# Weight frequencies of an FFT-style convolution prepared in five groups instead of six

## The chip, the cores and the metric

The kernel runs on one core of a Trainium2 chip. Its engines are TensorE (PE in the profile; PEld is its weight load), VectorE (DVE), ScalarE (ACT), GpSimd (POOL) and SyncE (SP, which issues most DMAs). The metric is the device time of one execution in microseconds (us). Before the change it is 263.42 us, the median of three runs from 263.04 to 263.55.

## The reference

A 7x7 convolution over a 224x224 image with 96 channels in and 96 out, written as a product of Fourier transforms. It wraps around at the edges.

```
Xf = rfft2(x, axes=(1, 2))                     # x: (1, 224, 224, 96) bf16
Wf = rfft2(pad(w, 224 x 224), axes=(0, 1))     # w: (7, 7, 96, 96) bf16
Yf = einsum('bhwi,hwio->bhwo', Xf, Wf)
y  = irfft2(Yf, s=(224, 224), axes=(1, 2)).astype(bf16)
```

## The kernel before

**What it computes.** Only the image's height is transformed. It is cut into 8 blocks of 28 rows, each with 6 rows of overlap, and a block's transform has 17 frequencies (`NS`). Frequencies 0 and 16 are real (`REAL`); each of the others has two parts and a third plane, their difference, for a complex product of three multiplications. Along the width the 7 taps are applied directly, two output columns at a time, in a form with ten tap planes (`NTAP`: seven taps and three sums). So the transformed weights WF have 2 + 3 x 16 = 50 slots of 10 planes of 96x96, and a product is a chain of matmuls of 96 columns, with data planes as the stationary operand and WF as the moving one.

**Tiles and rounds.** The width is cut into 7 tiles of 32 columns, t = 0 to 6. `b_round(t, s, mid, end, ...)` (L532) multiplies frequency s of tile t. It takes two banks of the eight in PSUM: b0 is filled by 19 matmuls, then the round's fillers (`mid()`) stand in TensorE's order, then b1 by 14 matmuls. ScalarE copies a part of b0 to `tt_`; VectorE makes u from b0 and `tt_`, later v from `tt_` and b1; GpSimd adds u and v into yf, which SP sends to DRAM. u, v and `tt_` have two buffers each (`tv`, L782). An inverse transform of each tile follows later (`c_jobs`) and reads yf back as `tt`.

**J planes.** VectorE makes the sums and differences of the data that the matmuls load, three frequencies at a time (`JGB`), some rounds ahead, in three operations (`jit`, L479). Operation 1 serves b1, operation 2 the first matmuls of b0, operation 3 the last ones of b0. In the rounds in which planes are made, GpSimd's sum waits until they are done.

**Tiles 0 and 1 together.** The first loop runs r = 0 to 20. Frequency r of tile 0 and frequency r - 4 of tile 1 (`LAG`) alternate, and the slots in which fillers are placed are numbered k = 2r + t from r = 4 on. `add(a, b, jobs)` registers jobs for the slots a to b - 1, and `pace` (L787) takes equally many from the list in each, rounded up. The fillers are the weight groups and the forward transforms (`f_jobs`, matmuls of `xn` with Fm, in parts of 8, 5 and 4 frequencies) of tiles 1 and 2.

**Weight preparation.** `PGRP` (L33) says which frequencies are prepared together. `prep_jobs(gi)` (L349) has two kinds of job:
- `mk_(ob)`: matmuls into one bank. The stationary operand is the raw weights `wq`, read with a step of 96 elements: 98 rows (49 taps, for output channels o and o + 48) and 128 columns, of which 96 are the input channels. The moving operand is a part of Em, the matrix of the transform: 2 x 20 columns for each frequency of the group. One matmul gives output channels o and o + 48; 48 matmuls make a group. One evacuation then writes the bank into WF as bf16, on VectorE or ScalarE, whichever `evac` (L119) counts as less loaded.
- `diff(s)`: the third plane of a frequency as a difference of the first two, one VectorE operation of 960 elements. A group's differences follow its last matmul job.

Group 0 (frequencies 0 and 1) is prepared at the start and has a form of its own, 128 columns and four matmuls to a bank. The other groups of before have 3 frequencies: 120 columns, four matmuls and 480 columns to a bank, 12 banks. Group gi is registered for the slots of the group ahead of it (L807): `add(2 * PGRP[gi - 1][0], 2 * PGRP[gi - 1][1] - 1, ...)`. That gives slots 0 to 2 (group 1), 4 to 8 (group 2), 10 to 14 (group 3), 16 to 20 (group 4) and 22 to 26 (group 5), three jobs to a slot in the last four. When r passes the second last group's end by one (L838), `wq`'s memory is given to the inverse transform's buffers, and GpSimd clears one of them, GX.

Banks, and the buffers of u, v and `tt_`, are handed out when the program is built; an instruction waits until the last user of its bank or buffer is done. Each engine works through its instructions in the program's order. All operations are recorded by one helper, so that the profile shows L88 for nearly all of them; they are told apart by tile names.

Of the kernel before, what the change touches and what calls it, by code (L numbers as in the profile page):

```python
# [27 lines left out]
NB = 8  # L28
# [1 line left out]
NTAP = 10  # L30
TAPS = ((7, 8, 9, 6), (0, 2, 4, 6), (1, 3, 5))
NSLOT = 2 + 3 * (NS - 1)
PGRP = ((0, 2), (2, 5), (5, 8), (8, 11), (11, 14), (14, 17))  # L33
YGRP = ((0, 3), (3, 6), (6, 9), (9, 12), (12, 15), (15, 17))
SA = 13
NB4 = 4
# [14 lines left out]
def slot(s, part):  # L51
    return part if s == 0 else 2 + 3 * (s - 1) + part
# [3 lines left out]
def kernel(  # L56
# [7 lines left out]
    _, H, W, C = x.shape  # L64
# [8 lines left out]
    C2 = C // 2  # L73
# [31 lines left out]
    def bank():  # L105
        return pools["psb"].tile([128, 512], F32, name="pb")
# [5 lines left out]
    def apart(key, zone, r):  # L112
        for z, q in parts.setdefault(key, []):
            if z != zone and q.engine != r.ins.engine:
                tc.declare_no_dep(r.ins, q, reason="disjoint parts of one tile")
        parts[key].append((zone, r.ins))
        return r

    def evac(out_ap, in_ap, n):  # L119
        if tail[0]:  # L120
            return tail_evac(out_ap, in_ap, n)
        cv, ca = 180 + 1.0 * n, 160 + 0.85 * n
        if load["v"] + cv <= load["a"] + ca:
            load["v"] += cv
            return VE.tensor_copy(out=out_ap, in_=in_ap)
        load["a"] += ca
        return SE.copy(out=out_ap, in_=in_ap)

    def tail_evac(out_ap, in_ap, n):
        tail[0] += 1  # L130
        return VE.tensor_copy(out=out_ap, in_=in_ap) if tail[0] % 2 else SE.copy(out=out_ap, in_=in_ap)
# [29 lines left out]
    xh_bufs = [late[:, 2 * (XW + 32) + i * XHW:2 * (XW + 32) + (i + 1) * XHW] for i in range(2)]  # L161
    assert 2 * (XW + 32 + XHW) <= 8 * NTAP * C and NSLOT - 8 > slot(PGRP[-1][0], 0)

# [185 lines left out]
    def prep_jobs(gi):  # L349
        s0, s1 = PGRP[gi]  # L350
        ns = s1 - s0
        full = gi == 0
        ncol = (NSLOT_OF(s0, s1) if full else 2 * ns) * NTAP
        nb = C // NB
        hb = NB // 2
        nr = 512 // NB if full else ncol
        assert ncol <= nr and NB * nr <= 512 and C2 % hb == 0

        def mk_(ob):
            def f():  # L360
                pw = bank()
                pv_ = pw[:, 0:NB * nr].rearrange("p (k h q) -> p k h q", h=2, q=nr)
                ev = Em[:, :, slot(s0, 0):slot(s1 - 1, 2) + 1, :]
                ev = Em.rearrange("p h a t -> p h (a t)")[:, :, 0:nr] if full else ev.rearrange("p h (s r) t -> p h s (r t)", r=3)[:, :, :, 0:2 * NTAP]
                for k in range(hb):
                    o = ob * hb + k
                    TE.matmul(pv_[:, k], lhsT=wqx[0:PW2, o:o + 127 * C + 1:C], rhs=ev, start=True, stop=True)
                pv_ = pv_[0:C]
                o0, o1 = ob * hb, (ob + 1) * hb
                wv = WF[0:C, slot(s0, 0):slot(s1 - 1, 2) + 1]  # L370
                if full:
                    wv = wv.rearrange("i a t (h o) -> i (a t) h o", h=2)
                    apart(("W", gi), ob, evac(wv[..., o0:o1], pv_[..., 0:ncol].rearrange("i k h q -> i q h k"), NB * ncol))
                    return
                wv = wv.rearrange("i (s r) t (h o) -> i s (r t) h o", r=3, h=2)
                apart(("W", gi), ob, evac(wv[:, :, 0:2 * NTAP, :, o0:o1],
                      pv_.rearrange("i k h (s q) -> i s q h k", s=ns), NB * ncol))
            return f

        def diff(s):  # L380
            def f():
                load["v"] += 60 + C * NTAP / 1.92
                w0, w1, w2 = (WF[0:C, slot(s, r)].rearrange("i t o -> i (t o)") for r in range(3))
                VE.tensor_tensor(out=w2, in0=w0, in1=w1, op=ALU.subtract)
            return f
        return [mk_(ob) for ob in range(nb)] + ([] if full else [diff(s) for s in range(s0, s1) if s not in REAL])

    def NSLOT_OF(s0, s1):
        return slot(s1 - 1, 2) + 1 - slot(s0, 0)
# [381 lines left out]
    for f in prep_jobs(0):  # L771
        f()
# [30 lines left out]
    def add(a, b, jobs):  # L803
        qs.append([a, b, jobs, len(jobs)])

    for gi in range(1, len(PGRP)):
        add(2 * PGRP[gi - 1][0], 2 * PGRP[gi - 1][1] - 1, prep_jobs(gi))  # L807
    for t in range(2):
# [10 lines left out]
    for r in range(NS + LAG):  # L819
# [10 lines left out]
        for p in range(3):  # L830
            if r == SH2[p + 1] + 1 - (p == 2):
# [5 lines left out]
                add(2 * r, 2 * r + (8, 7, 5)[p], fj[0] + fj[1])  # L837
        if r == PGRP[-2][1] + 1:  # L838
            assert not any(q[2] for q in qs[:len(PGRP) - 1])
            wtmp_cm.__exit__(None, None, None)  # L840
# [10 lines left out]
        for t in range(2):  # L851
            s = r - LAG * t
# [79 lines left out]
    for i, (j, h) in enumerate(order):  # L932
# [3 lines left out]
        k = i + 8 - LF  # L936
# [38 lines left out]
```

## Time and profile before

| | |
|---|---|
| median of three runs | 263.42 us |
| the profiled execution | 263.23 us |
| its span in the trace | 261.5 us |
| granted TensorE clock | 1.00 |
| TensorE's first to last weight-preparation matmul | 15.6 to 74.3 us |
| matmuls out of `wq` | 48 of 128 columns, 240 of 120 |
| evacuations 96x480 into WF | 51 on ScalarE (586 ns), 9 on VectorE (642 ns) |
| differences `WF<-WF` on VectorE | 14, 744 ns each |
| HBM traffic | 160 GB/s over the span |

Times are counted from the span's start. A group row gives busy time, mean length of one instruction, and the idle time ahead of them with what ended it. In a timeline a row is a run of like instructions of one engine: start, length, and in brackets the idle time ahead of it. Matmuls are pipelined and a row of them ends with the drain of the last one, so rows overlap; how long a matmul occupies TensorE is read from the start of one row to the start of the next.

### The profile page before, as it was taken

The page shows a single profiled execution, that of the slowest core. Times are in us where ns is not written, and L with a number is a line of the kernel's source. Part 1 is how long each engine was busy: PE and PEld are TensorE (multiplying, and loading weights), DVE is VectorE, ACT ScalarE, POOL GpSimd, SP SyncE. Part 2 cuts the span into 40 slices and gives each one's busy share as a digit, 9 for nine tenths or more (in the row PEclk, how much of TensorE's full clock was granted, in tenths as well). Part 3 has the DMA queues.
Part 4 walks back from the last instruction along what each step waited for, and adds up shares of the span by engine and source line. Part 5 has one row for each costly group of instructions (what it writes and reads, how often), then busy time and mean ns, then how long its engine had stood idle before and what let it go on. Part 6 is the DMA issues. An engine that isn't in the chain of part 4 may idle for free.

```text
span 261.5 us, 12201 instructions
## 1 busy us (share of the span) xinstructions
PE 251.8 (96%) x5156; PEld 233.9 (89%) x5156; DVE 213.9 (82%) x455; ACT 198.0 (76%) x499; POOL 106.7 (41%) x172
## 2 busy tenths in 40 slices
PE   8999998999999999999999999999999999999982
PEld 3679998999999999999999989998999999999861
DVE  5659999898878889877977797777978889889982
ACT  5548997678885667997988879988798886666662
POOL 7784223435546533432243313543143222555621
PEclk9999999999999999999999999999999999999999
DMA  6848010721112399997978469797969853495145
GB/s 171 238 136 205 23 49 3 231 89 50 46 52 88 99 274 144 271 275 200 300 207 238 127 184 262 204 241 181 288 215 207 221 174 133 132 174 169 53 115 177
DMA packets 41416, 43.44 MB, mean 166 GB/s; under 512 B 30836, under 2 KB 33104, under 8 KB 41362
## 3 DMA queue, kind: packets, MB, share of 16 engines
q1 hardware_dynamic: 41044, 41.98, 58.5%
q8 instruction: 40, 0.66, 1.2%
q0 software_dynamic: 192, 0.52, 0.7%
q10 hardware_dynamic: 126, 0.17, 0.2%
q14 instruction: 14, 0.11, 0.1%
HBM read 22.09 MB, written 19.66 MB: 160 GB/s over the span
## 4 chain that ended last, share of the span: by engine, by line
PE 84%; DVE 4%; issue 4%; ACT 3%; POOL 3%; POOLq 0%; DVEq 0%; ACTq 0%
PE pb L88 84%; POOL ct L88 2%; ACT WF L88 1%; DVE xf L88 1%; DVE J L88 1%; POOL yf L88 1%; ACT xf L88 1%; DVE wq L88 1%; DVE u L88 0%; DVE v L88 0%; DVE yf L88 0%; ACT tt L88 0%; ACT J L88 0%; ACT tt__5413 L88 0%; ACT tt__1159 L88 0%
## 5 line engine op out<-in xcount | busy, mean ns | idle before, releaser
L88 PE MATMUL pb<-WF,J 96*128 96x96 bf16 x2782 | 160.4, 206 | 0.1
L88 PEld LDWEIGHTS <-J 96*128 96x128 bf16 x2782 | 136.0, 98 | 8.2 <-DVE u L88 1.5
L88 POOL TENSOR_TENSOR yf<-v,u 128x384 bf16<-128x384 f32 x70 | 69.1, 1002 | 127.2 <-issue 69.1
L88 ACT CAST xf<-pb 96x408 bf16<-96x408 f32 (+2 forms) x147 | 68.8, 486 | 9.1 <-PE pb L88 7.3
L88 PE MATMUL pb<-WF,xf 96*128 96x96 bf16 x991 | 61.4, 206 | 0.8 <-ACT xf L88 0.5
L88 DVE TENSOR_TENSOR J<-xf 96x1824 bf16<-96x1824 bf16 (+1 forms) x82 | 56.9, 732 | 0.1
L88 PEld LDWEIGHTS <-xf 96*128 96x128 bf16 x991 | 48.8, 98 | 1.4 <-ACT xf L88 0.6
L88 PE MATMUL pb<-Fm,xn 118*128 118x136 bf16 (+3 forms) x640 | 45.5, 199 | 1.4 <-DVE u L88 0.8
L88 PEld LDWEIGHTS <-xn 118*128 118x128 bf16 x640 | 30.5, 97 | 1.8 <-issue 1.8
L88 PE MATMUL pb<-tt,Gm 102*84 102x384 bf16 (+1 forms) x132 | 32.1, 326 | 0.0
L88 ACT CAST WF<-pb 96x480 bf16<-96x480 f32 (+1 forms) x57 | 28.4, 576 | 4.6 <-PE pb L88 4.5
L88 ACT CAST yo<-pb 84x384 bf16<-84x384 f32 (+1 forms) x65 | 27.8, 483 | 2.9 <-PE pb L88 2.9
L88 ACT CAST J<-pb 84x384 bf16<-84x384 f32 (+1 forms) x65 | 28.0, 484 | 2.5 <-PE pb L88 2.5
L88 DVE TENSOR_TENSOR J<-J 96x912 bf16<-96x912 bf16 (+2 forms) x41 | 22.8, 555 | 0.0
L88 PE MATMUL pb<-wq 98*128 98x120 bf16 (+1 forms) x288 | 21.4, 226 | 0.1
L88 PEld LDWEIGHTS <-wq 98*128 98x128 bf16 x288 | 19.4, 148 | 0.6 <-issue 0.6
L88 POOL TENSOR_TENSOR xn<-v,u 128x384 bf16<-128x384 f32 x12 | 10.9, 924 | 9.4 <-DVE J L88 6.4
L88 DVE CAST WF<-pb 96x480 bf16<-96x480 f32 (+1 forms) x15 | 8.8, 613 | 4.2 <-PE pb L88 4.2
L88 PE MATMUL pb<-wu 128*128 128x512 bf16 x39 | 11.0, 444 | 1.1 <-DVE ct L88 1.1
L88 PEld LDWEIGHTS <-Gm 102*84 102x84 bf16 (+1 forms) x132 | 11.1, 117 | 0.8
L88 DVE TENSOR_TENSOR yf<-v,u 128x384 bf16<-128x384 f32 x20 | 11.2, 558 | 0.7
L88 ACT COPY xf<-xf 96x816 bf16<-96x816 bf16 (+3 forms) x18 | 10.3, 630 | 0.0
(406 smaller groups left out, 252.8 us busy)
## 6 DMA issues: line engine op xcount, KB each, us to landing
scr<-yf SPq DMA_DIRECT2D x30, 288.0 KB
xn<-in_x_dram SPq DMA_DIRECT2D x12, 672.0 KB
tt<-scr SPq DMA_DIRECT2D x24, 336.0 KB
out_dram<-yo SPq DMA_DIRECT2D x12, 252.0 KB
out_dram<-J SPq DMA_DIRECT2D x12, 252.0 KB
tt<-scr SPq DMA_DIRECT2D x6, 288.0 KB
WF<-in_x_dram SPq DMA_DIRECT2D x2, 672.0 KB
scr<-yf SPq DMA_DIRECT2D x6, 192.0 KB
```

Source lines behind the costliest of these rows:

```text
L88: r = fn(*a, **k)
```

## The change

`PGRP` has five groups instead of six: frequencies 8 to 11 and 12 to 16 take the place of three groups of 3. `prep_jobs` computes the number of matmuls to a bank from the moving columns: 3 of 160 columns (480 in the bank, 16 banks) for the group of 4, and 2 of 200 columns (400 in the bank, 24 banks) for the group of 5. Groups 0 to 2 come out as they were. By L807 the group of 4 falls into slots 10 to 14, with 16 matmul jobs and 4 differences, and the group of 5 into slots 16 to 22, with 24 matmul jobs and 4 differences, four jobs to a slot in both. `wq`'s memory is given away at r = 13 instead of 15.

```diff
-PGRP = ((0, 2), (2, 5), (5, 8), (8, 11), (11, 14), (14, 17))
+PGRP = ((0, 2), (2, 5), (5, 8), (8, 12), (12, 17))
...
-        nb = C // NB
-        hb = NB // 2
         nr = 512 // NB if full else ncol
-        assert ncol <= nr and NB * nr <= 512 and C2 % hb == 0
+        hb = 512 // (2 * nr)
+        nb = C2 // hb
+        assert ncol <= nr and C2 % hb == 0
...
-                pv_ = pw[:, 0:NB * nr].rearrange("p (k h q) -> p k h q", h=2, q=nr)
+                pv_ = pw[:, 0:2 * hb * nr].rearrange("p (k h q) -> p k h q", h=2, q=nr)
...
-                    apart(("W", gi), ob, evac(wv[..., o0:o1], pv_[..., 0:ncol].rearrange("i k h q -> i q h k"), NB * ncol))
+                    apart(("W", gi), ob, evac(wv[..., o0:o1], pv_[..., 0:ncol].rearrange("i k h q -> i q h k"), 2 * hb * ncol))
...
-                      pv_.rearrange("i k h (s q) -> i s q h k", s=ns), NB * ncol))
+                      pv_.rearrange("i k h (s q) -> i s q h k", s=ns), 2 * hb * ncol))
```

## The prediction

> **What bounds the kernel now.** I read the page's busy shares first, then the same shares by stage, then TensorE's timeline inside the stage that the change touches, then VectorE's timeline beside it.
>
> ```profile
> PE 251.8 (96%) x5156; PEld 233.9 (89%) x5156; DVE 213.9 (82%) x455; ACT 198.0 (76%) x499; POOL 106.7 (41%) x172
> ```
>
> ```profile
> 38.60:53.64 15.04, 14.28 (x345) 14.16 (x343) 13.29 (x26) 9.66 (x24) 4.98 (x5) 1.00 0.44 127
> 53.64:65.62 11.98, 11.88 (x267) 11.76 (x265) 10.62 (x22) 10.23 (x24) 5.93 (x6) 1.00 0.14 51
> 65.62:78.16 12.54, 12.50 (x283) 12.41 (x281) 10.34 (x21) 10.02 (x24) 5.91 (x6) 1.00 0.11 41
> ```
>
> TensorE (PE) sets the end: nearly full in every stage, clock 1.00, and after this stage (78 to 247 us) its timeline has hardly a gap. So what TensorE gains or loses before 78 us should come out at the end one for one. The second reading is the warning: VectorE (DVE) is 82 to 89% busy in these three stages. A busy share is no price, but a queue that full has little room for work that arrives in a lump.
>
> The stage in TensorE's timeline, then VectorE's:
>
> ```profile
> 67.23 0.93 PE L88 MATMUL pb<-WF,J 96*128 96x96 bf16 x18
> 68.00 0.50 PE L88 MATMUL pb<-WF,xf 96*128 96x96 bf16 x8
> 68.34 0.46 PE L88 MATMUL pb<-WF,J 96*128 96x96 bf16 x7
> 68.64 0.92 PE L88 MATMUL pb<-wq 98*128 98x120 bf16 x12
> 69.39 0.40 PE L88 MATMUL pb<-Fm,xn 118*128 118x64 bf16 x8
> 69.82 0.93 PE L88 MATMUL pb<-WF,J 96*128 96x96 bf16 x18
> ```
>
> ```profile
> 51.87 2.10 DVE L88 TENSOR_TENSOR WF<-WF 96x960 bf16<-96x960 bf16 x3
> 53.90 0.54 DVE L88 SCALAR_TENSOR_TENSOR v<-tt__1501,pb 128x384 f32<-128x384 f32 x1
> ```
> The columns are start, length, engine, operation, output<-input, shape, count. The first six rows are one round: 18 + 8 + 7 = 33 matmuls of 96 columns, the round's share of weight preparation (`wq`, three banks of four matmuls), then pieces of the next tile's transform (`xn`). A row's length holds the drain of its last matmul, so spacing is read from start to start. The last two show that three differences of weight planes (`WF<-WF`) hold VectorE for 2.03 us before it can empty round 14's second bank. I count rounds as the kernel counts slots: k = 2r + tile.
>
> **1. TensorE's work.** Spacings: 120 columns 0.75 us / 12 = 62.5 ns (68.64 to 69.39); 136 columns 60 ns (three from 99.39 to 99.57); 384 columns 165 ns (two from 105.31 to 105.64); 96 columns 42.6 ns (18 from 67.23 to 68.00). The line through 136 and 384 (0.423 ns a column) gives 120 columns 53.2 ns, so the weight matmuls are 9 ns above it. Group 0 tells why: 48 of 128 columns took 3.03 us (15.62 to 18.65), 63.1 ns, so 8 columns more cost 0.6 ns where the line asks for 3.4. The weight load sets the spacing; its group's mean is 148 ns against 98 ns for loads from J or xn. Once the matmul is longer than the load, it is the line that counts: 160 columns 70.2 ns, 200 columns 87.1 ns. Both shapes are absent from this trace, so these are estimates.
>
> Removed: 144 x 62.5 = 9.00 us (three groups of 48). Added: 48 x 70.2 + 48 x 87.1 = 3.37 + 4.18 = 7.55 us. Gain 1.45 us. Bounds: if the 9 ns excess stayed, 48 x (79.5 + 96.4) = 8.44 us, gain 0.56; if spacing stayed at 62.5 ns, gain 3.0. I take the line, since its two ends bracket both widths.
>
> The Trainium skill (TensorE: Matmul & The Clock Gate, "Weight-path perf modes — Fast Weight Load (FWL) and DoubleRow") speaks against any gain here: it has the fast load on for 128 weights not in fp32, with a column step up to 1,024 elements, and this load's step is 96. By it the old matmuls would already sit on the line (144 x 53.2 = 7.66 us) and the gain would be 0.1 us. The trace disagrees: 62.5 ns and 148 ns against 98.
>
> **2. Evacuations.** 36 of 480 elements become 16 of 480 and 24 of 400. On ScalarE (ACT) three of 480 take 1.47 us with 0.59 for one, so 0.445 us apart; two of 320 take 0.77 with 0.43 for one, 0.335 apart; 400 lies at 0.39 between. 36 x 0.445 = 16.0 becomes 16.5 us, and the built program puts 36 of the 40 on ScalarE. Their output now goes in runs of 3 and 2 elements instead of 4. No row here has such a run; in contiguous rows and runs of 4 the length follows the element count alone (84x384 contiguous 484 ns, 96x400 494, 96x408 500). I take no penalty; below nothing is excluded, since no run shorter than 4 can be an easier write; the upper end is in the rivals.
>
> **3. What moves.** Rounds 10 to 13 prepare 48 matmuls as before, but in four banks each instead of three. All of group 4 falls into rounds 16 to 21 (8 matmuls, four banks each), rounds 22 to 25 lose their 12 each. The differences come four at a time: in round 14 (three before) and in round 22 (before: three in round 20, two in round 26). The GpSimd (POOL) memset of GX moves from 15 to 13 in the frequency loop: 0.56 us on an engine that is 41% busy. SP's transfers keep their order. Until round 22 TensorE therefore carries more, 3.37 - 3.0 + 4.18 - 3.0 = +1.55 us; the 3.0 us back come after it.
>
> **4. New waits.** I followed banks and buffers through the built program's instruction order, with durations of before (u 0.27 us apart, v 0.46, a difference 0.68; the two first J operations 1.32, or 1.63 to 1.88 beside a POOL sum as at 55.09 and 40.65; the third 0.54). All of these are estimates.
> - Round 10: the fourth bank moves the round's second half onto the bank that VectorE's yf sum empties at 40.73 us; TensorE would be there at 40.5. +0.3.
> - Round 11: TensorE already waits 0.76 us for u (43.48). The bank in question is now asked for two banks earlier, but freed at the same time. +0.1.
> - Round 16: the second half's bank is emptied by round 14's v, which stands behind four differences. TensorE arrives at 54.9, v ends at about 55.7. +0.8. Queued behind that v are u, v, round 15's J planes and, through them, GpSimd's sums (they wait for planes).
> - Round 18: a u behind those planes; 0.4 in place of the 0.3 of before (58.67 to 58.94). +0.1, and 0.1 of small ones.
> - Rounds 22 to 27: the largest. J planes for round 27 are made in round 24. Before, the VectorE queue between round 21's planes and these held only u and v, and it idled:
>
> ```profile
> 71.99 0.36 DVE L88 SCALAR_TENSOR_TENSOR u<-pb,tt__2113 128x192 f32<-128x192 f32 x1 [0.51 <-ACT tt__2113 L88]
> 73.02 0.56 DVE L88 SCALAR_TENSOR_TENSOR v<-tt__2113,pb 128x384 f32<-128x384 f32 x1 [0.66 <-PE pb L88]
> 73.49 1.40 DVE L88 TENSOR_TENSOR J<-xf 96x1824 bf16<-96x1824 bf16 x2
> ```
>
> (The bracket is the idle time ahead of the row and its cause: 0.51 + 0.66 us, so the planes were not late.) Now it holds planes 1.9, u 0.3, four differences 2.7, v, u, v 1.2, a wait for GpSimd's sum to free u 0.3, u, v 0.7, the next planes' first two 1.4: 8.5 us, starting 0.7 us after TensorE's round 21 ends, so 9.2. TensorE, lightened of its `wq` matmuls, reaches round 27 after four rounds of 1.64 and one of 1.41: 8.0 us. It waits 1.2 us.
>
> Sum: -1.45 + 0.3 + 0.1 + 0.8 + 0.2 + 1.2 = +1.15; the 0.2 us wait at 69.82 (69.39 + 8 x 28.75 ns, the spacing from 67.00 to 67.23, = 69.62) falls away: **+0.95 us**. After round 27 VectorE has no differences left and TensorE has no slack to give the time back. The profiled execution took 263.23 us (span 261.5 and 1.7 around it), 0.19 below the median 263.42; so 264.2 for it and **264.4** for the median.
>
> **Rivals.**
> - *Faster: the waits are hidden.* If VectorE reached round 14's v and round 24's planes 1 us sooner, only part 1 stays: -1.45 + 0.2 of small waits, 262.2. It decides at round 27: the planes must be ready 8.0 us after round 21's end instead of 9.2. For it: TensorE is 96% busy and VectorE had 1.2 us idle there. Against: the differences are 2.7 us.
> - *Even.* Round 16's wait is halved, round 27's only 0.6 us: 263.4.
> - *Short writes cost.* Rounds 18 to 21 give ScalarE 0.31 (tt) + 4 x 0.39 + 0.47 (xf) = 2.34 us against TensorE's 33 x 42.6 ns + 8 x 87.1 ns + 0.23 = 2.33. With no slack, 0.1 us more per evacuation is 0.4 us a round, 1.6 us in all: 266.0.
> - *Spacing keeps its excess*, 0.56 instead of 1.45 gained: up to 265.3. The Trainium skill's rule (fast load on) would leave no work gained, 265.8; with the 62.5 ns against it I give that 0.02, inside this case.
> - *The change does nothing it says*: excluded; the built program has 240 weight loads from `wq` where there were 288, and 64 evacuations into WF outside group 0 where there were 60.
>
> **Chances.** Forecast (264.0 to 265.0) 0.42; short writes 0.10; spacing 0.10; even 0.14; faster 0.24. Within 0.2% means within 0.53 us, about what a measurement here can tell from no change: same 0.14, faster 0.24, slower 0.62. The range takes most of the faster case and the short writes: 262.1 to 266.2. The slower cases alone: 264.0 to 266.2.
>
> **What would show it.** Part 1: twelve `wq` matmuls of 160 columns 0.84 us, eight of 200 columns 0.70 us, start to start. Part 2: the 96x400 casts near 494 ns. Part 4: TensorE waits for VectorE at two places, some 0.8 us eight matmuls of 200 columns into the stage (for a v) and some 1.2 us six rounds after the last `wq` (for J). If neither is there, the forecast fails and the time is near 262.2.

## The result and the profile after

The changed kernel takes **269.99 us** (median of six executions, 268.60 to 272.06) against 263.26 us before (six, 262.75 to 263.55): a ratio of 1.0264, 95% interval 1.0233 to 1.0295. That is 6.7 us slower; forecast was 264.4, with 266.2 as the upper end. The profiled execution took 268.60 us (span 266.8), 5.37 more than that of before.

The busy shares of the page, then the shares by stage. The stage is cut where TensorE stands at the same work as in the three rows of before: the `xf` matmuls ahead of round 10's weight matmuls, those weight matmuls of round 16, the `xf` matmuls of round 22, those of round 28.

```profile
PE 252.9 (95%) x5108; PEld 233.7 (88%) x5108; DVE 215.1 (81%) x456; ACT 203.7 (76%) x502; POOL 107.0 (40%) x172
```

```profile
38.60:56.29 17.69, 15.67 (x346) 15.11 (x343) 14.08 (x27) 15.21 (x27) 4.96 (x5) 1.00 0.40 117
56.29:72.25 15.96, 14.62 (x268) 13.60 (x265) 11.55 (x25) 14.19 (x32) 6.93 (x7) 1.00 0.11 40
72.25:83.74 11.49, 9.73 (x235) 9.47 (x232) 10.70 (x20) 5.35 (x13) 3.95 (x5) 1.00 0.07 27
```

The columns are the stretch and its length, then busy time and count of TensorE, its weight loads, VectorE, ScalarE and GpSimd, then clock, DMA share and GB/s. On the page nothing seems to happen: TensorE 251.8 us before and 252.9 after, 96 and 95% of the span. By stage the loss is plain. The stretch up to round 16 has 346 matmuls where it had 345, but lasts 17.69 us instead of 15.04, and ScalarE's busy time there rises from 9.66 to 15.21 us while its count rises from 24 to 27. The second takes 15.96 us instead of 11.98, with 268 matmuls where it had 267 and ScalarE busy for 14.19 us instead of 10.23; the third, with its `wq` matmuls gone, comes 1.05 us shorter (11.49). The clock is 1.00 throughout.

TensorE's timeline of the changed kernel, all rows of the stage at which the view shows a wait (start, length, shape, count, idle time ahead and what ended it):

```profile
43.41 0.60 PE L88 MATMUL pb<-wq 98*128 98x160 bf16 x6 [0.57 <-ACT WF L88]
44.17 0.38 PE L88 MATMUL pb<-wq 98*128 98x160 bf16 x3 [0.15 <-ACT WF L88]
...
55.83 0.33 PE L88 MATMUL pb<-WF,xf 96*128 96x96 bf16 x4 [1.10 <-DVE WF L88]
...
57.99 0.93 PE L88 MATMUL pb<-WF,J 96*128 96x96 bf16 x18 [0.78 <-DVE v L88]
...
76.64 0.33 PE L88 MATMUL pb<-WF,xf 96*128 96x96 bf16 x4 [0.78 <-DVE WF L88]
...
82.12 0.34 PE L88 MATMUL pb<-WF,J 96*128 96x96 bf16 x4 [0.98 <-DVE J L88]
```

The two waits that were forecast are there, 0.78 us for a v at round 16 and 0.98 us for J planes at round 27. So are waits for casts and for differences, which were not. ScalarE's timeline shows why, first one row of before, then the changed kernel:

```profile
40.69 1.47 ACT L88 CAST WF<-pb 96x480 bf16<-96x480 f32 x3
```

```profile
40.69 3.43 ACT L88 CAST WF<-pb 96x480 bf16<-96x480 f32 x4
...
50.47 3.55 ACT L88 CAST WF<-pb 96x480 bf16<-96x480 f32 x4
53.74 0.70 ACT L88 CAST xf<-pb 96x512 bf16<-96x512 f32 x1
54.26 0.49 ACT L88 ACTIVATE tt__1509<-pb 128x288 f32<-128x288 f32 x1
...
58.36 2.11 ACT L88 CAST WF<-pb 96x400 bf16<-96x400 f32 x4
```

Before, three casts of 96x480 took 1.47 us. Here four take 3.43 and 3.55 us, where 4 x 0.445 + 0.14 = 1.92 would be in line. The four of 96x400 come every 0.49 us, with 0.39 to be expected from their element count. Behind the second four of 96x480 the `tt` of round 14 is late (54.26), and VectorE stands idle for 1.69 us until it comes, where it was 0.58 us before. VectorE's row of before, then of the changed kernel:

```profile
51.60 0.36 DVE L88 SCALAR_TENSOR_TENSOR u<-pb,tt__1501 128x192 f32<-128x192 f32 x1 [0.58 <-ACT tt__1501 L88]
```

```profile
54.85 0.36 DVE L88 SCALAR_TENSOR_TENSOR u<-pb,tt__1509 128x192 f32<-128x192 f32 x1 [1.69 <-ACT tt__1509 L88]
```

**The theory** after this reading (A): the casts now write runs of 3 and 2 bf16 elements, and such short runs are slow; the lateness runs from ScalarE through `tt` to u, the differences and v. Rivals: PSUM is read in another step and that is slow (C); or the four differences in a lump do all of it and the casts are late only behind them (B).

### The profile page after: what moved, and what is told of

It reads as the page before. It is cut to its first block, busy times and chain, and to the rows that moved or that the text cites. A ratio compares the mean times of both kernels' runs of the same rounds, so it can differ in the third digit from the quotient of the medians.

```text
span 266.8 us, 12109 instructions
## 1 busy us (share of the span) xinstructions
PE 252.9 (95%) x5108; PEld 233.7 (88%) x5108; DVE 215.1 (81%) x456; ACT 203.7 (76%) x502; POOL 107.0 (40%) x172
## 4 chain that ended last, share of the span: by engine, by line
PE 73%; DVE 7%; ACT 7%; issue 4%; DMA 4%; SPq 2%; POOL 1%; DVEq 0%; ACTq 0%
PE pb L88 73%; ACT WF L88 5%; DVE J L88 2%; DMA wq<-in_w_dram 2%; DVE WF L88 2%; SPq L88 2%; DMA wq<-wq 1%; DVE v L88 1%; ACT xf L88 1%; DVE xf L88 1%; POOL yf L88 1%; DVE u L88 0%; DVE yf L88 0%; ACT tt L88 0%; ACT tt__1159 L88 0%
## 5 line engine op out<-in xcount | busy, mean ns | idle before, releaser
L88 POOL TENSOR_TENSOR yf<-v,u 128x384 bf16<-128x384 f32 x70 | 69.8, 1010 | 131.9 <-issue 69.7
L88 ACT CAST xf<-pb 96x408 bf16<-96x408 f32 (+3 forms) x146 | 69.1, 492 | 8.7 <-PE pb L88 6.9
L88 ACT CAST WF<-pb 96x480 bf16<-96x480 f32 (+1 forms) x59 | 35.7, 748 | 4.7 <-PE pb L88 4.6
L88 PE MATMUL pb<-wq 98*128 98x120 bf16 (+3 forms) x240 | 21.0, 234 | 1.2 <-ACT WF L88 0.7
L88 PEld LDWEIGHTS <-wq 98*128 98x128 bf16 x240 | 18.3, 145 | 2.2 <-issue 2.1
L88 DVE CAST WF<-pb 96x480 bf16<-96x480 f32 (+1 forms) x17 | 10.9, 679 | 4.2 <-PE pb L88 4.1
(404 smaller groups left out, 252.9 us busy)
```

Source lines behind the costliest of these rows:

```text
L88: r = fn(*a, **k)
```

## The experiments

Profiled executions start their first preparing matmul at 15.6 to 18.0 us, as the first DMAs land, and that goes straight through to the end. So profiles are compared by a **stretch**: from the second block of preparing matmuls (the first 20 of 120 columns) to the start of the 25 `J` matmuls of round 27. Before it is 77.09 - 20.55 = 56.54 us. All versions beside each other (ratios with 95% intervals, each against the kernel before on the same chip):

| version | median us | ratio | stretch us |
|---|---|---|---|
| before | 263.26 | 1 | 56.54 |
| changed | 269.99 | 1.0264 [1.0233, 1.0295] | 62.12 |
| `contig` | 266.07 | 1.0121 [1.0079, 1.0163] | 58.01 |
| `changed_pairs` | 265.86 | 1.0118 [1.0071, 1.0166] | 58.03 |
| `runs2` | 267.27 | 1.0174 [1.0147, 1.0202] | 60.15 |
| `spread` | 269.54 | 1.0255 [1.0221, 1.0289] | 61.85 |
| `old_slots` | 269.74 | 1.0258 [1.0210, 1.0306] | 60.40 |
| `contig_old_slots` | 264.52 | 1.0057 [1.0037, 1.0076] | 56.37 |
| `pairs_old_slots` | 264.89 | 1.0068 [1.0044, 1.0092] | 56.43 |
| `pairs_early` | 266.11 | 1.0122 [1.0077, 1.0168] | 58.22 |
| `pairs_no_differences` | 262.99 | 0.9994 [0.9979, 1.0008] | 55.67 |
| `pairs_pool4` | 268.47 | 1.0211 [1.0188, 1.0234] | 60.37 |
| `pairs_pool2` | 268.51 | 1.0206 [1.0181, 1.0231] | 58.22 |
| `before_pairs` | 263.19 | 0.9993 [0.9970, 1.0017] | 56.59 |

In the three versions with `old_slots` in their names a wait of 1.19 us follows in round 28, after the stretch. `before_runs3` and `before_runs1` ran once each and stand in their own section. A stretch is one profiled execution; a median can differ from its profile by more than a microsecond, so that small differences are read from the stretches and not from the medians.

### The writes alone: `contig`

```diff
-                wv = wv.rearrange("i (s r) t (h o) -> i s (r t) h o", r=3, h=2)
-                apart(("W", gi), ob, evac(wv[:, :, 0:2 * NTAP, :, o0:o1],
+                if ns > 3:
+                    z = 2 * hb * 2 * NTAP
+                    wo = wv.rearrange("i (s r) t o -> i s (r t o)", r=3)[:, :, ob * z:(ob + 1) * z].rearrange("i s (q h k) -> i s q h k", h=2, k=hb)
...
+                apart(("W", gi), ob, evac(wo,
```

The groups of 4 and 5 are written as runs of 120 and 80 elements. The weights land at other places than the products expect, so this version does not compute the convolution; its work is the same.

> The changed kernel, but each bank of the groups of 4 and 5 is written into WF as runs of 120 or 80 neighbouring elements instead of 3 or 2: same reads from PSUM, same counts, same engines, same order (the weights land at permuted places, so the output is not the reference's). Theory A, short write runs slow ScalarE's evacuations: the casts of 480 fall from 0.81 to about 0.45 us start to start, those of 400 from 0.49 to about 0.40, and the time comes to the forecast made without a penalty, about 264.4 us (263.8 to 265.5). Theory C, the wider step between PSUM reads (640 and 800 bytes instead of 480) slows them: casts and time as in the changed kernel, 269 to 270. Theory B, only the placement of the differences and the denser rounds: 269 to 270 as well, with the same casts.

ScalarE's casts in `contig`:

```profile
41.00 1.92 ACT L88 CAST WF<-pb 96x480 bf16<-96x480 f32 x4
...
56.16 1.66 ACT L88 CAST WF<-pb 96x400 bf16<-96x400 f32 x4
```

Four casts take 1.92 us, the value in line with before, with the changed kernel's read of PSUM. C falls, and B as the only cause: the differences still come four at a time, yet the stretch shrinks by 4.1 us and the time by 3.9. The median, 266.07 us, still lies above the range that A had given (263.8 to 265.5), so short writes are not the whole of the loss. What TensorE still waits for in `contig`:

```profile
43.79 0.60 PE L88 MATMUL pb<-wq 98*128 98x160 bf16 x6 [0.68 <-DVE u L88]
...
55.79 0.93 PE L88 MATMUL pb<-WF,J 96*128 96x96 bf16 x18 [0.21 <-DVE v L88]
...
58.94 0.33 PE L88 MATMUL pb<-WF,J 96*128 96x96 bf16 x4 [0.25 <-DVE u L88]
...
72.85 0.33 PE L88 MATMUL pb<-WF,xf 96*128 96x96 bf16 x4 [0.54 <-DVE WF L88]
...
78.34 0.34 PE L88 MATMUL pb<-WF,J 96*128 96x96 bf16 x4 [0.99 <-DVE J L88]
```

### What a short run costs: `before_runs3`, `runs2`, `before_runs1`

`before_runs3` puts 3 matmuls into a bank in place of 4 in before's last three groups; `runs2` puts 2 instead of 3 into a bank in the changed kernel's group of 4; `before_runs1` lets before's last three groups write the two halves of the channels innermost, which makes every element a run of its own. The names behind # are added here.

```diff
-        hb = NB // 2
+        hb = 3 if gi > 2 else NB // 2                                   # before_runs3
...
-        hb = 512 // (2 * nr)
+        hb = 2 if ns == 4 else 512 // (2 * nr)                          # runs2
...
-                wv = wv.rearrange("i (s r) t (h o) -> i s (r t) h o", r=3, h=2)
+                wv = wv.rearrange("i (s r) t (h o) -> i s (r t) o h", r=3, h=2)   # before_runs1
```

> The kernel before with three instead of four matmuls to a bank in groups 3 to 5: 16 casts of 360 elements in runs of 3 for 12 of 480 in runs of 4, PSUM step 480 bytes as before. By the length of 320 (0.335) and 480 elements (0.445) a cast of 360 would come every 0.36 us. Theory A: it takes clearly more, 0.55 to 0.65 us, and the time rises by some us. Theory C: 0.36 us, time within 1 us of before.

> The changed kernel with two instead of three matmuls to a bank in the group of 4: 24 casts of 320 elements in runs of 2, all starting on a multiple of 4 bytes, for 16 of 480 in runs of 3, half of which start in the middle of such a word. If odd runs are what costs (A, by alignment): 0.40 us each, 9.6 us for 12.9, and 2 to 3 us less than the changed kernel: 266.5 to 268. If every run costs the same extra time whatever its length (A, by count: 160 runs in a cast in both): 0.335 + 0.36 = 0.70 us each, 16.7 us for 12.9, and slower than the changed kernel: 272 or more.

> Complete kernel: the kernel before, where in groups 3 to 5 (fill 10 on) the 36 evacuations of 480 elements write single elements, 48 elements apart, in place of runs of 4; the read of PSUM takes the same pairs of steps in the other order. A look at the cost of single elements. If the cost goes by writes that do not fill and start on 4 bytes (runs of 2: 1.21 ns an element; runs of 3, of which every other one is off the 4 bytes: 1.68): about 2.3 to 3 ns an element, a spacing of 1.1 to 1.5 us on ScalarE, and 275 to 290 us. If the cost goes by the number of runs alone at the 2.4 ns a run that runs of 2 show: 2.4 ns an element, 1.15 us, the same to a measurement; if by bytes alone: 0.45 us and 263 us. Runs of 3 at 1.68 above runs of 2 at 1.21 speak against cost by the number of runs alone.

ScalarE in `before_runs3`, in `runs2` and in `before_runs1`:

```profile
41.73 2.66 ACT L88 CAST WF<-pb 96x360 bf16<-96x360 f32 x4
```

```profile
40.93 2.53 ACT L88 CAST WF<-pb 96x320 bf16<-96x320 f32 x6
```

```profile
41.06 6.67 ACT L88 CAST WF<-pb 96x480 bf16<-96x480 f32 x3
```

The spacing on ScalarE, start to start and as a mean, is 0.60 us for 360 elements in runs of 3 and 0.80 for 480 in the changed kernel, 0.39 for 320 and 0.487 for 400 in runs of 2, some 2.1 for 480 single elements, 0.445 for 480 in runs of 4. For one element: 1.7 ns in runs of 3, 1.2 in runs of 2, some 4.4 alone, 0.93 in runs of 4. For one run: 5.0 ns for 3 elements, 2.4 for 2, 4.4 for 1 and 3.7 for 4. A run of 3 is dearer than a run of 2 and than a run of 4, so it is neither a price for each run nor one for each element.

The place of a run counts too. The last two groups of `before_runs3` are all on ScalarE, 16 casts each. In both, the casts of the channels from 6, 15, 30 and 39 come 0.69 to 0.76 us ahead of the next one; the others do so by 0.56 to 0.67, and the first of each block of casts by 0.52. Those four are the only ones whose runs of 3, 6 bytes long, straddle a multiple of 16 bytes, counted from the start of a plane. Among the others an odd first channel is no dearer than an even one. What sets the price beyond that was not tried.

`before_runs3` made the kernel before 8.5 us slower (271.2 us, one execution, against 262.67) with no change to its groups, waits by ScalarE's casts all along: the short writes do the damage by themselves. `before_runs1` took 318.49 us, more than any theory said; a part of that is the clock (mean 0.89, see the end), and much of the rest is TensorE's waits for casts, of up to 1.82 us each.

### The differences one at a time: `spread`

The differences of the group of 4 go to slots 14 to 17, those of the group of 5 to 22 to 25, and `wq`'s memory is given away two frequencies later.

```diff
+            for i in range(n):
+                add(2 * s0 - 2 + i, 2 * s0 - 1 + i, jobs[len(jobs) - n + i:len(jobs) - n + i + 1])
```

> The changed kernel with one difference per round (rounds 14 to 17 and 22 to 25) instead of four in rounds 14 and 22, and wq's memory given away two frequencies later, as before. Theory B: TensorE's waits of 1.1, 0.8, 0.8 and 1.0 us at rounds 16, 24 and 27 vanish and the time falls by most of the loss, to 264 or less. Theory A: ScalarE's casts stay at 0.81 and 0.49 us, so only the part of the waits behind the differences goes, 1.5 to 3 us: 266.5 to 268.5.

It gained nothing (269.54 us, above the ranges of both theories), and the reason was new. VectorE, then GpSimd, in `spread`:

```profile
55.23 0.64 DVE L88 TENSOR_TENSOR WF<-WF 96x960 bf16<-96x960 bf16 x1
...
56.53 1.42 DVE L88 TENSOR_TENSOR WF<-WF 96x960 bf16<-96x960 bf16 x1
...
60.47 1.46 DVE L88 TENSOR_TENSOR WF<-WF 96x960 bf16<-96x960 bf16 x1
```

```profile
56.42 1.01 POOL L88 TENSOR_TENSOR yf<-v,u 128x384 bf16<-128x384 f32 x1 [1.82 <-DVE v L88]
60.41 1.00 POOL L88 TENSOR_TENSOR yf<-v,u 128x384 bf16<-128x384 f32 x1 [2.98 <-issue]
```

The same difference takes 0.64 us alone and 1.42 or 1.46 us when one of GpSimd's sums begins just ahead of it. Of the changed kernel's lumps of four (2.35 and 3.16 us) at most one difference can have met a sum; one difference in each round nearly always does. The Trainium skill (SBUF — State Buffer, "Who interferes with whom") says that a VectorE instruction with two inputs in SBUF contends with a GpSimd instruction that reads SBUF; the trace agrees, with 0.8 us more for VectorE and GpSimd's 1.0 us unchanged.

### The places alone and with cheap writes: `old_slots`, `contig_old_slots`

Every difference goes to its place of before or close to it: 12 and 13 stand in slot 22 and not 20, because their matmuls end in slot 21.

```diff
+                k = {8: 14, 9: 14, 10: 14, 11: 20, 12: 22, 13: 22, 14: 26, 15: 26}[s0 + i]
+                add(k, k + 1, jobs[len(jobs) - n + i:len(jobs) - n + i + 1])
...
-        if r == PGRP[-2][1] + 1:
+        if r == PGRP[-2][1] + 3:
```

> The changed kernel with its short writes (runs of 3 and 2) kept, and only the eight differences put into before's places (8, 9, 10 in fill 14; 11 in fill 20; 12, 13 in 22; 14, 15 in 26), as in the two versions with cheap writes that gave ratios of 1.0057 and 1.0068. Theory (the writes cost some 3 us whatever the places of the differences): 267.0 to 269.5 us, ratio 1.015 to 1.025, with four casts of the group of 4 still at 3.2 to 3.5 us and TensorE waits on ScalarE's casts of 0.4 to 0.8 us in rounds 11 and 16 to 20. Rival (writes and places cost only together, since the casts are late only behind the bunched differences): 264.5 to 265.5 us, ratio 1.005 to 1.009.

> Contiguous writes (weights at permuted places, so the output is not the reference's) and the differences back in the slots of before: three in round 14, one in 20, two in 22, two in 26; wq's memory is given away at r = 15 as before. If what is left above before with contiguous writes (3.4 us in the medians) is the lump of four differences: the waits of 0.54 us (round 24, for a difference) and 0.99 us (round 27, for J) vanish, those at rounds 16 and 18 stay under 0.5 us together, and with 0.9 us gained in TensorE's matmuls the time is 262 to 263.5, level with before. If the lump is not the cause, it stays at 265 to 266.5.

With the short writes kept, before's places change nothing that can be measured in the time (269.74 us): the stretch is 1.7 us shorter, but 1.19 us of that come back as the wait in round 28. With long writes they bring the time from 266.07 to 264.52 and the stretch from 58.01 to 56.37 us; 262 to 263.5 us had been expected. In the trace the wait for J planes in round 27 is gone, that of 0.54 us in round 24 stays, and one of 1.19 us in round 28 is new.

### Long writes in a complete kernel: `changed_pairs`, `pairs_old_slots`, `before_pairs`

One matmul now prepares channels o and o + 1 instead of o and o + 48 (the second copy of the raw weights is shifted by one element instead of 48), so that a bank with 3 or 2 matmuls writes runs of 6 or 4.

```diff
-                    o = ob * hb + k
+                    o = 2 * (ob * hb + k)
...
-                wv = wv.rearrange("i (s r) t (h o) -> i s (r t) h o", r=3, h=2)
+                wv = wv.rearrange("i (s r) t (o h) -> i s (r t) o h", r=3, h=2)
```

> The changed kernel with the channel pairs alone (runs of 6 and 4, differences four at a time as in the change). Theory A and the lump: as with contiguous writes, 264.5 to 266.5, with TensorE waiting 0.5 to 1 us each at rounds 24 and 27. If run length were not what mattered: 269 to 270.

> The changed kernel, complete, with channels o and o + 1 instead of o and o + 48 made by one matmul (the second half of wq shifted by 1 column instead of 48), so that a bank is written in runs of 6 and 4 elements instead of 3 and 2, and with the differences in the slots of before. Theory A: casts of 480 in runs of 6 and of 400 in runs of 4 cost 0.45 to 0.50 and 0.39 us, as contiguous ones do, and the time is that of the contiguous writes with the same slots, 262 to 263.5. If only aligned runs of 8 bytes are free, the runs of 6 (12 bytes) keep part of the loss: 0.6 us a cast and 264 to 266. If the copy shifted by 2 bytes is slow, the first weight matmul starts later than 15.7 us and everything with it.

> The kernel before with the channel pairs: runs of 8 instead of 4 elements, nothing else. Theory A with runs of 4 already free: casts of 480 stay at 0.445 us, the time within 0.6 us of before (262.2 to 263.8), unless the shifted copy delays the first weight matmul. If runs of 4 still cost something: 0.40 us or less per cast and up to 1 us gained.

`changed_pairs` repeats `contig` (58.03 and 58.01 us of stretch), `pairs_old_slots` repeats `contig_old_slots`, and `before_pairs` equals before. So from 4 elements on a run costs no more than a long one (480 elements every 0.45 us, 400 every 0.38, as in `contig`), and the short writes cost some 4 us: over the stretch 62.12 - 58.03 = 4.09 us with the change's places and 60.40 - 56.43 = 3.97 us with before's; in the medians 4.1 and 4.9.

### Where the saved work goes: `pairs_early`, `pairs_no_differences`

Still 264.89 us, though TensorE has less to do. `pairs_early` prepares the group of 5 in slots 14 to 19 and puts every difference at before's slot or earlier.

```diff
-                k = {8: 14, 9: 14, 10: 14, 11: 20, 12: 22, 13: 22, 14: 26, 15: 26}[s0 + i]
+                k = {8: 14, 9: 14, 10: 14, 11: 20, 12: 20, 13: 20, 14: 23, 15: 26}[s0 + i]
```

> Complete kernel, on the version with neighbouring channels (runs of 6 and 4 elements, free of extra cost): the 24 matrix jobs of the group of 5 are spread over fills 14 to 19, where before's fourth group stood, instead of 16 to 21, and the differences stand exactly where before has them or earlier: 8, 9, 10 in fill 14, 11, 12, 13 in fill 20, 14 in fill 23, 15 in fill 26. Theory (all that is left of the loss against before are the two waits on the differences, 0.54 us in round 24 and 1.19 us in round 28, less the TensorE work saved): both waits go, the 0.68 us wait in round 11 stays or is shared with before's 0.76 us there, and the time comes 1.2 to 1.7 us below that version: 262.3 to 263.4 us, ratio to before 0.996 to 1.001; round 27's end relative to the first preparing matmul falls to 60.3 to 61.0 us against 61.5 before. Rival (the matmuls saved buy nothing because VectorE or GpSimd work sets the rounds' pace, so another wait takes the place): 264 to 265 us, ratio 1.004 to 1.007, with new TensorE waits of over 1 us together between rounds 14 and 28.

The theory behind it failed: TensorE's waits moved and grew.

```profile
72.06 0.33 PE L88 MATMUL pb<-WF,xf 96*128 96x96 bf16 x4 [0.41 <-DVE WF L88]
...
76.02 0.34 PE L88 MATMUL pb<-WF,J 96*128 96x96 bf16 x4 [0.86 <-DVE J L88]
...
81.99 0.34 PE L88 MATMUL pb<-WF,J 96*128 96x96 bf16 x4 [1.08 <-DVE J L88]
```

VectorE's queue holds the planes behind the differences, and from 66.9 to 84.2 us it idles 1.3 us in all; in the same rounds of before (61.3 to 78.55 us) it was 2.8. `pairs_no_differences` asks whether that is the bound: four of the differences are left out, and their planes are zero.

```diff
-                k = {8: 14, 9: 14, 10: 14, 11: 20, 12: 22, 13: 22, 14: 26, 15: 26}[s0 + i]
+                k = {8: 14, 9: 14, 10: 14, 11: 20}.get(s0 + i)
+                if k:
+                    add(k, k + 1, jobs[len(jobs) - n + i:len(jobs) - n + i + 1])
+                else:
+                    add(6, 7, [lambda s=s0 + i: GE.memset(WF[0:C, slot(s, 2)], 0.0)])
```

> Incomplete on purpose of the question: the version with neighbouring channels and the differences in before's places, but the four differences of frequencies 12 to 15 are left out, and GpSimd writes zeros in their planes in fill 6. Every other instruction and its place stay. Theory (VectorE sets the pace in rounds 22 to 28, where before leaves it idle for some 2.6 us in all and that version for 0.8 us; the four differences are what it has no time for, so the TensorE work saved comes back as waits on them): the waits of 0.54 us in round 24 and 1.19 us in round 28 go and nothing takes their place, the stretch from the second block of preparing matmuls (the first with 120 columns) to the last product of the inverse transform falls from 231.3 us to 229.3 to 230.1 us (before: 230.7), and the time is 262.2 to 263.6 us, ratio 0.996 to 1.001. Rival (the sums u, v, J and GpSimd's yf set the pace whatever the differences): waits on v or J of over 0.8 us in all come in rounds 22 to 28, the stretch stays above 230.6 us, ratio 1.003 to 1.007.

Of the waits that the view shows only the 0.68 us of round 11 is left, and the stretch is 55.67 us, 0.87 less than before. Row by row, what is left of smaller waits (some 0.2 us each in rounds 10 and 18) is about as much as the small waits of before, so 0.87 us is what the saved matmuls are worth in TensorE's own time. Yet the median of this incomplete version, 262.99 us and so in the range expected, only ties with before (0.9994).

### The differences on GpSimd: `pairs_pool4`, `pairs_pool2`

```diff
+                gk = {12: 21, 13: 22, 14: 24, 15: 25}.get(s0 + i)       # pairs_pool2: {14: 24, 15: 25}
...
+                        GE.tensor_tensor(out=w2, in0=w0, in1=w1, op=ALU.subtract)
```

> Complete kernel: the version with neighbouring channels and before's places, but the differences of frequencies 12 to 15 are computed by GpSimd, in fills 21, 22, 24 and 25, and not by VectorE. Theory (VectorE has no time for them in rounds 22 to 28, and that is all that holds the saved TensorE work back): if GpSimd's own idle stretches of 1.2 to 2.6 us take them, at an estimated 1.3 to 2.6 us each (its sum of 384 elements a partition takes 1.0 us, this one has 960 at half the bytes), round 27 comes as in the version without them, 55.7 to 56.2 us after the second block of preparing matmuls against 56.5 before, and the time is 262.5 to 263.5 us. Rival (the four only move: GpSimd's yf sums queue behind them, and VectorE's u and J behind those, or VectorE's J sums slow down beside them): waits of over 1 us in all on VectorE's u, v or J in rounds 22 to 28, round 27 at 56.5 us or later, 264 to 266 us.

> Complete kernel: as the one with four differences on GpSimd, but 12 and 13 stay with VectorE in fill 22, and only 14 and 15 go to GpSimd, in fills 24 and 25. Theory: the wait of 1.19 us in round 28 goes, the 0.54 us in round 24 stays; round 27 as in the version with before's places, 56.2 to 56.6 us after the second block of preparing matmuls; 263.0 to 264.2 us. Rival (GpSimd late with yf): a new wait of 0.5 us or more before round 30, 264.2 to 266 us.

The rival held, and by more than it had said: 268.47 us against 264 to 266. VectorE, then GpSimd, then TensorE in `pairs_pool4`:

```profile
75.89 0.36 DVE L88 SCALAR_TENSOR_TENSOR u<-pb,tt__2109 128x192 f32<-128x192 f32 x1 [2.09 <-POOL yf L88]
76.17 0.54 DVE L88 SCALAR_TENSOR_TENSOR v<-tt__2109,pb 128x384 f32<-128x384 f32 x1
76.63 3.26 DVE L88 TENSOR_TENSOR J<-xf 96x1824 bf16<-96x1824 bf16 x2
```

```profile
72.91 2.00 POOL L88 TENSOR_TENSOR WF<-WF 96x960 bf16<-96x960 bf16 x1
74.87 1.94 POOL L88 TENSOR_TENSOR yf<-v,u 128x384 bf16<-128x384 f32 x2
76.78 2.85 POOL L88 TENSOR_TENSOR WF<-WF 96x960 bf16<-96x960 bf16 x1
```

```profile
79.95 0.50 PE L88 MATMUL pb<-WF,J 96*128 96x96 bf16 x4 [3.73 <-DVE J L88]
80.25 0.84 PE L88 MATMUL pb<-WF,xf 96*128 96x96 bf16 x8
80.89 2.20 PE L88 MATMUL pb<-WF,J 96*128 96x96 bf16 x25
```

A difference on GpSimd takes 2.00 us alone and holds up the yf sums, for which u waits 2.09 us; and where it meets VectorE's two J operations, these take 3.26 us instead of 1.40, and GpSimd 2.85. So the bound in these rounds is not VectorE's time alone but the chain of u, v, yf, differences and J planes through two engines that slow each other. `pairs_pool2` missed both its ranges as well (268.51 us): TensorE waits 1.65 us for J planes at round 27, where `contig` waited 0.99.

```profile
79.26 0.34 PE L88 MATMUL pb<-WF,J 96*128 96x96 bf16 x4 [1.65 <-DVE J L88]
```

## Why the prediction was wrong

The step that failed is **step 2, the evacuations**: "in contiguous rows and runs of 4 the length follows the element count alone", and "I take no penalty" for runs of 3 and 2. All rows at hand had runs of 4 or more; the rule was carried past the shortest run that the trace showed. The extra is 0.35 us a cast in runs of 3 (0.80 against 0.445) and 0.10 us in runs of 2 (0.487 against 0.383). The rival for it had 0.1 us a cast and 1.6 us in all, in rounds 18 to 21. For the group of 5 with its runs of 2 that was nearly right: from the `xf` matmuls of round 18 to those of round 22 the changed kernel takes 10.92 us (61.33 to 72.25), `runs2` as much, `changed_pairs` 9.59, so 1.33 us. It missed the runs of 3 of the group of 4: from round 10 to round 18 the changed kernel takes 22.73 us (38.60 to 61.33), `runs2` 20.80 and `changed_pairs` 20.22, so 2.5 us, from rounds 10 to 13 on, where it had seen no danger.

Point by point, over the stretch:

- **Part 1, TensorE's work**: forecast 1.45 us, measured 0.87 (`pairs_no_differences` against before). The spacings of the trace, raw start to start, give the same: 62.9 ns for 120 columns, 74.7 for 160 and 95.0 for 200 (means of the blocks without a wait), so 48 x (3 x 62.9 - 74.7 - 95.0) = 0.91 us. The line through 136 and 384 columns had 70.2 and 87.1. It was drawn through other matmuls (data with a step of 1, other moving operands), and the excess of 9 ns that the `wq` matmuls had at 120 columns did not vanish but fell to 4.5 and grew to 8; so the step "once the matmul is longer than the load, it is the line that counts" did not hold for these matmuls. By the Trainium skill's rule (TensorE: Matmul & The Clock Gate, "Weight-path perf modes — Fast Weight Load (FWL) and DoubleRow"), under which the fast load was on all along, the gain was estimated at 0.1 us; the measured 0.87 does not agree with that, and the loads from `wq` still take 145 ns on average in the changed kernel.
- **Part 3, what moves**: as foreseen.
- **Part 4, new waits**: forecast +2.4 us, and without the short writes nearly that. From start to start in `contig`: round 10 +0.26 (0.3 forecast), round 11 -0.08 (+0.1), round 16 +0.39 (+0.8), round 18 +0.10 (+0.2), round 27 +1.15 (+1.2); round 24 waits 0.70 us for a difference, which was not foreseen; the 0.2 us at 69.82 went. Sum 2.32 us; 2.32 - 0.87 = 1.45, and the stretch grew by 58.01 - 56.54 = 1.47. So the rows explain this version's profile, and over the stretch the forecast would have been 0.5 us low for it, by part 1. That waits and saved work come out so near to each forecast is in part luck: rounds 16 and 24 missed by 0.4 and 0.7 us in opposite directions.
- **The signs** misled in one place. "Some 0.8 us for a v" at round 16 came out at 0.78 us in the changed kernel, but `contig` shows only 0.21 of it from the lump of differences. The rest is ScalarE, whose casts delayed `tt`, and with it the u ahead of those differences, by an idle 1.69 us on VectorE (0.81 in `contig`). The sign of part 2 told it apart: casts of 96x400, forecast near 494 ns, took 742 (573 in `contig`).
- **The rivals**: the faster one, in which the waits hide, is what `pairs_no_differences` comes nearest to, and even that is 263.0, not 262.2. The rival of short writes had the right cause with 266.0 us, for the part of it that lies in rounds 18 to 21.

The sum of the loss over the stretch, +5.58 us: -0.87 for TensorE's work, +2.3 for the waits behind differences and lighter rounds, +4.1 for the short writes. After the stretch the two profiles run in step (251.27 - 77.09 = 174.18 and 256.46 - 82.67 = 173.79 us to the last inverse product).

**What stays open.** The changed kernel's median lies 1.4 us above its profiled execution, and its executions spread by 3.5 us where before's spread by 0.8 (in a later series of 17 executions before's spread by 3.4 as well, 262.31 to 265.69). `contig`'s median lies 1.3 us above its profile too, so the rows explain its stretch and not the whole 3.4 us of its median against before on the same chip. The longer executions have a lower mean clock (0.981 at 272.06 us, 0.996 at 268.60), but they have no trace. Two things could lower the clock. One is the start: in the profile of `pairs_early`, which lies 2.7 us above that version's median, an input DMA lands late, TensorE waits 2.31 us, the clock is 0.50 from 19.5 to 22.9 us, and the first 48 weight matmuls take 4.08 us instead of 3.03:

```profile
17.97 4.28 PE L88 MATMUL pb<-wq 98*128 98x128 bf16 x48 [2.31 <-DMA WF<-in_x_dram]
```

The other is a wait in the rounds that now and then grows, as that of 1.65 us in `pairs_pool2` does. Which of them it was in the changed kernel is not shown. None of the versions beats before: with cheap writes and before's places 1.0068 is left, and where the differences could go without a wait was not found.

## What to carry to other kernels

When an edit changes how many results share a bank, look at the run that the evacuation then writes: on ScalarE here, bf16 runs of 3 and 2 cost 1.8 and 1.3 times as much an element as runs of 4, and a rule read from the rows at hand, such as a length that follows the element count alone, holds only for the shapes that the trace has. TensorE's saved time was worth nothing here, where the next engine had no slack: measure that by leaving the other engine's work out before building a schedule around it. And a forecast sign that is met is no proof of its cause; ask what else would give the same wait.

## What the hardware showed beyond that

- VectorE pays for short runs too: in the changed kernel its casts of 96x480 took 922 to 1124 ns in runs of 3, against 642.
- A run of 3 on ScalarE costs more where it straddles a multiple of 16 bytes (0.69 to 0.76 us for 360 elements against 0.56 to 0.67).
- A two-input operation of 960 bf16 elements on VectorE takes 0.64 us, and 1.42 to 1.46 us when one of GpSimd's two-input sums starts just ahead.
- A TensorE wait of 3.73 us in `pairs_pool4` halves the clock, so that 25 matmuls took 2.20 us instead of 1.23:

```profile
76.00:79.95 3.95, 0.22 (x7) 0.07 (x3) 3.95 (x5) 0.41 (x1) 3.64 (x2) 0.82 0.19 75
79.95:82.00 2.05, 2.05 (x26) 2.05 (x27) 1.62 (x5) 0.26 (x1) 1.44 (x2) 0.50 0.03 8
82.00:84.00 2.00, 2.00 (x28) 2.00 (x26) 0.41 (x1) 0.71 (x3) 2.00 (x2) 0.50 0.00 0
84.00:86.00 2.00, 2.00 (x45) 2.00 (x43) 1.50 (x3) 1.04 (x3) 1.43 (x2) 0.66 0.34 134
```

The column after GpSimd's is the granted clock. Finer windows put the fall at 78.5 us, 2.3 us into the wait, and the return at 85.3, so that half the clock lasts 6.8 us. A shorter wait does it too: behind the 1.65 us of `pairs_pool2` the clock falls at 80.8 us, 1.6 us after TensorE has begun again (79.26), and returns at 84.2:

```profile
80.00:81.00 1.00, 1.00 (x27) 1.00 (x25) 0.56 (x3) 0.41 (x2) 1.00 (x2) 0.92 0.06 16
81.00:82.00 1.00, 1.00 (x16) 1.00 (x14) 0.73 (x2) 0.57 (x3) 1.00 (x1) 0.50 0.00 0
```

A wait of 1.10 us in the changed kernel and one of 1.59 us at the start of `before_pairs` left it at 1.00. The Trainium skill (TensorE: Matmul & The Clock Gate, "What's actually happening") puts the fall to half at an idle window of some 3.4 us and the return at as long a busy one. The lengths at half clock agree (3.4 us in `pairs_pool2` and `pairs_early`, twice that in `pairs_pool4`); the fall does not, since here waits of 1.65 and 2.31 us, and 2.3 us of a longer one, were enough.
